# Small transfers of 5 to 15 rows in the load stream of a decode step, with sixteen more from GpSimd

## The chip, the cores and the metric

The kernel runs on one core of one Trainium2 chip. The metric is device time in microseconds (us), from the launch to the end on that core. The profile's "span" is the part of it from the first to the last instruction.

The engines are named as in the profile: PE is TensorE (matmul), PEld its weight load, DVE VectorE, ACT ScalarE, POOL GpSimd, SP SyncE. A "q" behind the name (SPq) is the engine's own instruction queue, from which it issues DMA transfers.

## The reference

One decode step of a layer with attention and a gated feed-forward side by side, for two sequences (B = 2), one token each, all in float32:

```
xn  = layernorm(x)                                   # x: 2 x 1 x 512
q   = xn @ wq                                        # 512 x 4096: 32 heads of 128
k,v = the last 4096 of 32768 positions of the caches # 8 key/value heads, 4 query heads to each
A   = softmax(q k^T / sqrt(128)) v @ wo              # wo: 4096 x 512
g,u = xn @ W_gate, xn @ W_up                         # 512 x 1792 each
B   = (g * (g > 0) * u) @ W_down                     # 1792 x 512
out = x + A + B
```

Every weight and every used cache row is read once. Key and value rows are 2 x 8 x 4096 x 128 floats each, 67.1 MB together; the weights are about 27.8 MB.

## The kernel before

**What is loaded.** The attention is cut into four groups g = 0 to 3 (NG): one sequence and four of its key/value heads each. A group's keys come in two loads of 4096 KB, a = 0 and 1, two heads each, and its values likewise. So there are eight loads `k{g}_{a}` and eight `v{g}_{a}`, made by `load_kv` (L108). The weights come as `wq0`, `wq1` (L75), `wg`, `wu` (L79), `wd` (L92: one large transfer and four of 64 KB, two of which go to the tile `wx`), `wo0` in one piece and `wo1` in four (L482 to L485).

**The ring.** All big loads go into one pool of four buffers (`ring`, RING = 4), in the order of the code, each into the buffer of the load four before it. `load` (L69) allocates the buffer and calls `nc.sync.dma_start`, so SyncE issues all of them, one after the other, into one DMA queue. SyncE first waits until the buffer's last reader is done: for a k buffer the last transpose (L302), for a v buffer the last matmul of L379. Only the input x (`x2`, L128) is loaded by ScalarE.

**The order of the loads** is that of the code, written out by hand (`manual_schedule`): x2, wq0, wq1, wg, wu; k0_0, k0_1; then k1_0, v0_0, k1_1, v0_1; k2_0, v1_0, k2_1, v1_1; k3_0, v2_0, k3_1, v2_1; then v3_0, v3_1, wd with its small parts, wo0, wo1. The framework puts in the waits: an instruction that touches a tile, or a part of it, waits for earlier ones that touch the same part, and the end of a transfer is told by a semaphore.

**The work on a load.** A k buffer is transposed on PE in blocks of 128 x 128 (`transposes`, L294, 64 of them), DVE and ACT copy the results out of PSUM in turn (L291), and `scores` (L308) multiplies with q. `softmax` (L321) of the group before runs between the transposes of the next group's first k load. `values` (L372) multiplies the probabilities with a v buffer, `gather` and `finish` put the heads together, and `project` (L464) accumulates the output from wd, then wo0 and wo1. One copy (L489) and one transfer (L490) end the kernel.

**GpSimd** sets constants up at the start (L90 to L183). Later it has one instruction, the memset of part of wd's tile (L98).

Of the kernel before, what the change touches and what calls it, by code (L numbers as in the profile page):

```python
# [9 lines left out]
F32 = mybir.dt.float32  # L10
# [10 lines left out]
def kernel(  # L21
# [12 lines left out]
    nc = tc.nc  # L34
# [14 lines left out]
    NG = B * R  # L49
# [9 lines left out]
    const = ctx.enter_context(tc.tile_pool(name="const", bufs=1))  # L59
# [9 lines left out]
    def load(name, src, shape):  # L69
        t = ring.tile(shape, F32, name=name, tag="ring")  # L70
        nc.sync.dma_start(t, src)
        return t
# [19 lines left out]
    def load_down():  # L92
# [12 lines left out]
                nc.sync.dma_start(dst[32 * h:32 * h + 16].rearrange("p s e -> p (s e)"), low)  # L105
        return t

    def load_kv(cache, name, g, a):  # L108
        r, b = divmod(g, B)
        base = cache[b, r * C + 2 * a, SK - W:SK, :]  # L110
        run = J * DH
        src = bass.AP(
            tensor=cache.tensor, offset=base.offset, ap=[[run, PK], [SK * DH, 2], [1, run]]
        )
        return load(f"{name}{g}_{a}", src, [P, run])
# [91 lines left out]
    for kc in range(KC):  # L207
        m, k = divmod(kc, 2)
# [7 lines left out]
    for kc in range(KC):  # L216
        for r in range(R):
            for c in range(C):
                n = r * C + c
# [214 lines left out]
    for a in range(NP):  # L434
        kwork(0, a, load_kv(k_cache, "k", 0, a))
    for g in range(1, NG):
        for a in range(NP):
            kt_in = load_kv(k_cache, "k", g, a)
            v_in = load_kv(v_cache, "v", g - 1, a)
            kwork(g, a, kt_in, [softmax(g - 1)] if a == 0 else [])  # L440
            if a:
                gather(g - 1, a - 1)
            elif g % B == 1 and g > 1:
                spread_heads((g - 2) // B)
            values(g - 1, a, v_in)
        gather(g - 1, NP - 1)
        finish(g - 1)
    g = NG - 1
# [70 lines left out]
```

## Time and profile before

| | us |
|---|---|
| median of 2 runs (231.06 to 231.21) | 231.13 |
| the profiled execution | 231.12 |
| its span | 229.3 |
| PE busy | 184.7 |
| DVE busy | 67.4 |
| ACT busy | 48.4 |
| POOL busy | 7.7 |
| mean granted TensorE clock | 0.933 of full speed |

Busy times count an engine's own work; waits and the issuing of transfers are not in them. The slices of the page give the busy share of an engine in tenths for each fortieth of the span, and for DMA the mean over the core's 16 DMA engines. In a list of waits a row reads: who waited, at which line, for whom, us in total, how many times, the longest. In an order of time a row reads: start, length, engine, line, operation, output and input, and how many instructions were put together in the row, so that its length reaches from the start of the first to the end of the last.

### The profile page before, as it was taken

The numbers are of one execution on the slowest core, as the hardware profiler recorded it, in microseconds if no ns is written. First come the engines' busy times: TensorE is split into PE (matmuls) and PEld (weight loads), VectorE is DVE, ScalarE is ACT, GpSimd is POOL, SyncE is SP. The second block draws the span as 40 slices with busy tenths as digits, with TensorE's granted clock in tenths as the row PEclk, the third lists the DMA queues.
The fourth block names the chain that finished last, engine by engine and source line by source line (L and its number), as shares of the span: only waits on it lengthen the run. The fifth ranks groups of instructions, "written<-read, shape, count | busy, mean of one in ns | idle before, by whom it ended". The sixth has DMA issues, their size and how long they took to land.

```text
span 229.3 us, 4136 instructions
## 1 busy us (share of the span) xinstructions
PE 184.7 (81%) x1868; PEld 112.5 (49%) x1868; DVE 67.4 (29%) x137; ACT 48.4 (21%) x81; POOL 7.7 (3%) x26
## 2 busy tenths in 40 slices
PE   0096753859999889998999799599999974988694
PEld 0061220239666573664574565338656532247582
DVE  0500101033544462441473341147224224001000
ACT  2000100004444461540252331025234202010000
POOL 8200000000000000000000000000000100000000
PEclk9999987575999999999999999979999998599979
DMA  7999999999899999999999999999999999999991
GB/s 275 457 412 415 465 400 432 434 457 443 383 449 452 410 412 457 432 406 437 452 417 410 452 423 437 423 446 423 414 446 426 429 429 437 418 440 420 409 369 51
DMA packets 3856, 95.15 MB, mean 415 GB/s; under 512 B 438, under 2 KB 446, under 8 KB 768
## 3 DMA queue, kind: packets, MB, share of 16 engines
q1 hardware_dynamic: 3836, 94.90, 96.7%
q8 instruction: 14, 0.23, 0.4%
q14 instruction: 2, 0.02, 0.0%
q10 hardware_dynamic: 4, 0.00, 0.0%
HBM read 94.90 MB, written 0.00 MB: 414 GB/s over the span
## 4 chain that ended last, share of the span: by engine, by line
PE 53%; DMA 34%; DVE 5%; POOL 2%; ACT 2%; issue 1%; SPq 0%; POOLq 0%
DMA k<-in_A_k_cache_dram 24%; PE pk L302 23%; PE s L315 11%; DMA wo<-in_A_wo_dram 10%; PE o L379 9%; PE q_ps L220 2%; PE pp L359 2%; PE xt_ps L210 2%; ACT p L348 2%; PE oa L395 2%; DVE kT L291 1%; PE y_ps L466 1%; PE op L409 1%; DVE on L291 1%; DVE pt L360 1%
## 5 line engine op out<-in xcount | busy, mean ns | idle before, releaser
L302 PE MATMUL pk<-ident,k 128*128 128x128 f32 x512 | 68.2, 287 | 4.8 <-DMA k<-in_A_k_cache_dram 4.8
L302 PEld LDWEIGHTS pk<-ident,k 128*128 128x128 f32 x512 | 58.1, 146 | 19.8 <-issue 15.6
L291 DVE COPY kT<-pk 128x512 f32<-128x512 f32 x64 | 44.2, 691 | 50.7 <-PE pk L302 40.7
L291 ACT COPY kT<-pk 128x512 f32<-128x512 f32 x64 | 37.5, 586 | 80.1 <-PE pk L302 80.1
L315 PE MATMUL s<-kT,qz 128*32 128x512 f32 x256 | 32.1, 617 | 0.0
L379 PE MATMUL o<-v,pt 128*32 128x512 f32 x256 | 32.0, 633 | 0.0
L379 PEld LDWEIGHTS o<-v,pt 128*32 128x32 f32 x256 | 11.2, 116 | 15.4 <-issue 10.7
L315 PEld LDWEIGHTS s<-kT,qz 128*32 128x32 f32 x256 | 7.2, 112 | 12.8 <-issue 12.4
L210 PE MATMUL xt_ps<-rep,xn 2*128 2x32 f32 x16 | 3.7, 400 | 11.1 <-DVE xn L204 11.1
L466 PE MATMUL y_ps<-wo,oT 128*17 128x128 f32 x256 | 9.6, 311 | 2.9 <-DMA wo<-in_A_wo_dram 2.5
L395 PE MATMUL oa<-on,pick 128*16 128x128 f32 x64 | 8.3, 273 | 4.1 <-DVE on L291 3.3
L291 DVE COPY on<-o 128x512 f32<-128x512 f32 x4 | 2.8, 691 | 30.0 <-PE o L379 30.0
L395 PEld LDWEIGHTS oa<-on,pick 128*16 128x16 f32 x64 | 5.8, 97 | 11.1 <-DVE on L291 7.0
L220 PE MATMUL q_ps<-wq,xnT 128*32 128x512 f32 x64 | 9.0, 716 | 2.5 <-DMA wq<-in_A_wq_dram 2.0
L466 PEld LDWEIGHTS y_ps<-wo,oT 128*17 128x17 f32 x256 | 7.9, 111 | 4.5 <-DMA wo<-in_A_wo_dram 3.4
L247 PE MATMUL u_ps<-wu,xnT 128*32 128x448 f32 x32 | 5.8, 908 | 4.7 <-DMA wu<-in_B_W_up_dram 4.7
L210 PEld LDWEIGHTS xt_ps<-rep,xn 2*128 2x128 f32 x16 | 3.6, 319 | 11.0 <-issue 11.0
L291 ACT COPY on<-o 128x512 f32<-128x512 f32 x4 | 2.3, 586 | 26.6 <-PE o L379 26.6
L348 ACT ACTIVATE p<-s,nm 128x1024 f32<-128x1024 f32 x4 | 4.5, 1115 | 12.6 <-DVE nm L343 12.5
L359 PE MATMUL pp<-ident,p 128*128 128x128 f32 x32 | 5.1, 289 | 2.4 <-ACT p L348 1.5
L247 PE MATMUL g_ps<-wg,xnT 128*32 128x448 f32 x32 | 4.9, 774 | 2.5 <-DMA wg<-in_B_W_gate_dram 2.5
L98 POOL MEMSET wd<- 64x1024 f32 x1 | 0.9, 945 | 171.5 <-PE pk L302 171.5
(80 smaller groups left out, 68.3 us busy)
## 6 DMA issues: line engine op xcount, KB each, us to landing
k<-in_A_k_cache_dram SPq DMA_DIRECT2D x8, 4096.0 KB, 26.6
v<-in_A_v_cache_dram SPq DMA_DIRECT2D x8, 4096.0 KB, 27.1
wq<-in_A_wq_dram SPq DMA_DIRECT2D x2, 4096.0 KB, 21.4
wo<-in_A_wo_dram SPq DMA_DIRECT2D x1, 4096.0 KB, 30.9
wg<-in_B_W_gate_dram SPq DMA_DIRECT2D x1, 3584.0 KB, 29.4
wu<-in_B_W_up_dram SPq DMA_DIRECT2D x1, 3584.0 KB, 38.6
wd<-in_B_W_down_dram SPq DMA_DIRECT2D x1, 3328.0 KB, 26.9
wo<-in_A_wo_dram SPq DMA_DIRECT2D x1, 2048.0 KB, 19.9
```

Of the source, the lines that this page charges most:

```text
L210: nc.tensor.matmul(xt_ps[:, o, kc, :], cols, rep.rearrange("r s b -> r (s b)"), start=True, stop=True)
L220: nc.tensor.matmul(q_ps[r][32 * c:32 * c + 32, :], xnT[:, 0, kc, :], wqt[kc // 2][:, kc % 2, n * 512:(n + 1) * 512], start=(kc == 0), stop ...
L247: nc.tensor.matmul(dst[32 * c:32 * c + 32, :], xnT[:, 1, kc, :], wt[:, kc, c * FQ:(c + 1) * FQ], start=(kc == 0), stop=(kc == KC - 1),)
L291: (nc.vector.tensor_copy if turn[0] % 2 else nc.scalar.copy)(dst, src)
L302: nc.tensor.transpose(pk[:, u * P:(u + 1) * P], kt_in[:, j * P:(j + 1) * P], ident)
L315: nc.tensor.matmul(ss[g][32 * q:32 * q + 32, :], qz[:, g, 32 * n:32 * n + 32], kt[:, h, q * 512:(q + 1) * 512], start=(a == 0 and s1 == 0 ...
L348: nc.scalar.activation(p, both, AF.Exp, bias=nm, scale=SCALE, accum_out=l)
L359: nc.tensor.transpose(pp[:, u], pv[:, lo:lo + P], ident)
L360: nc.vector.tensor_tensor(pts[g][:, jh].rearrange("p n u k -> p u n k"), pp.rearrange("p u (n k) -> p u n k", k=HK), own.rearrange("p h i ...
L379: nc.tensor.matmul(o[32 * q:32 * q + 32, :], pts[g][:, jh, n].rearrange("p u k -> p (u k)"), v[:, lo:lo + 512], start=(s1 == 0 and jh == 0 ...
L395: nc.tensor.matmul(oa[g], pick[:, u, 8 - 8 * a:24 - 8 * a], ons[a][:, u], start=(a == 0 and u == 0), stop=(a == NP - 1 and u == 3),)
L466: nc.tensor.matmul(y_ps[32 * e:32 * e + 17, :], lhsT.rearrange("p b s -> p (b s)")[:, 0:17], w[:, e * P:(e + 1) * P], start=False, stop=stop,)
```

## The change

Two small tiles are added, `marks` and `gmarks`, and a function `mark`, which `load_kv` calls ahead of seven of its loads: k0_0, k1_0, k2_0, k3_0, v2_0, v3_0 and v3_1. Each call issues eleven transfers on SyncE's queue, of 5, 6, ... 15 rows from wq into slots of their own in `marks`; a row has 2 to 12 floats, 8 to 48 bytes. The slots are the same at each of the seven calls. The third and the fifth call (ahead of k2_0 and of v2_0) issue eight more each from GpSimd, of two rows of 2 to 9 floats, into `gmarks`. That makes 77 transfers on SyncE and sixteen on GpSimd. No instruction reads the two tiles. Nothing else is changed.

```
+    marks = const.tile([16, 11, 12], F32, name="marks")
+    gmarks = const.tile([2, 8, 12], F32, name="gmarks")
+    at = [0]
+
+    def mark():
+        for k in range(5, 16):
+            nc.sync.dma_start(marks[0:k, k - 5, 0:k - 3], wq[0:k, 0:k - 3])
+        if at[0] in (2, 4):
+            for n in range(8):
+                nc.gpsimd.dma_start(gmarks[:, n, 0:2 + n], wq[0:2, 0:2 + n])
+        at[0] += 1
+
     def load_kv(cache, name, g, a):
+        if name == "k" and a == 0 or (name, g, a) in (("v", NG - 1, 0), ("v", NG - 1, 1), ("v", NG - 2, 0)):
+            mark()
         r, b = divmod(g, B)
         base = cache[b, r * C + 2 * a, SK - W:SK, :]
```

## The prediction

> **What bounds the kernel now.** I read the page first: the summary, the slices, the queues and the chain.
>
> ```profile
> span 229.3 us, 4136 instructions
> PE 184.7 (81%) x1868; PEld 112.5 (49%) x1868; DVE 67.4 (29%) x137; ACT 48.4 (21%) x81; POOL 7.7 (3%) x26
> ...
> DMA  7999999999899999999999999999999999999991
> ...
> q1 hardware_dynamic: 3836, 94.90, 96.7%
> ...
> PE 53%; DMA 34%; DVE 5%; POOL 2%; ACT 2%; issue 1%; SPq 0%; POOLq 0%
> ```
>
> The chain gives PE the larger share, but it runs through PE because PE frees the ring buffers; the slices say what sets the time. All 94.90 MB come in on SyncE's one queue (q1), whose packets fill 96.7% of the span. DMA stands at 9 in 37 of 40 slices. So an interval in which that queue is empty goes straight onto the end, unless the queue was idle there anyway, and it hardly ever is.
>
> Next the table of windows, for the steady rate, the start-up and the run-out of the stream. Its columns are length, busy time of PE, PEld, DVE, ACT and POOL, clock, DMA share and GB/s.
>
> ```profile
> 0.00:10.00 10.00, 0.00 (x0) 0.00 (x0) 2.49 (x13) 1.58 (x2) 6.74 (x25) 1.00 0.90 358
> 50.00:220.00 170.00, 153.04 (x1427) 97.59 (x1431) 59.35 (x103) 45.66 (x77) 0.94 (x1) 0.94 1.00 428
> 221.00:225.50 4.50, 3.83 (x132) 3.00 (x123) 0.00 (x0) 0.00 (x0) 0.00 (x0) 1.00 0.63 252
> ```
>
> The steady rate is 428 GB/s, so a 4096 KB load (4.19 MB) takes 9.8 us of the stream. In the same 170 us the stream brings 428 x 170 = 72.8 MB, 17.3 loads, for 153.0 us of PE: 8.8 us of PE for each load. PE is a tenth faster than the stream and waits for it.
>
> How far ahead the stream is fed stands among the DMA issues (KB each, us from issue to landing) and in SyncE's own waits.
>
> ```profile
> k<-in_A_k_cache_dram SPq DMA_DIRECT2D x8, 4096.0 KB, 26.6
> ...
> wu<-in_B_W_up_dram SPq DMA_DIRECT2D x1, 3584.0 KB, 38.6
> wd<-in_B_W_down_dram SPq DMA_DIRECT2D x1, 3328.0 KB, 26.9
> ```
>
> ```profile
> SPq L71 <- PE pk L302: 93.3, 9, 14.0
> ...
> SPq L485 <- DMA wd<-in_B_W_down_dram: 4.0, 1, 4.0
> ```
>
> A load lands 26.6 us after its issue and needs 9.8 us itself, so there are 1 to 2 loads in the queue ahead of it. SyncE mostly stands waiting for PE to free a buffer, and it can afford that as long as it isn't held until the queue has run out.
>
> The last row is the one that decides here. L485 issues the pieces of wo. SyncE's order in time:
>
> ```profile
> 178.95 0.53 SPq L97 DMA_DIRECT2D wd<-in_B_W_down_dram  x1
> 179.53 1.50 SPq L105 DMA_DIRECT2D wx<-in_B_W_down_dram  x2
> 181.07 1.30 SPq L105 DMA_DIRECT2D wd<-in_B_W_down_dram  x2
> ...
> 201.07 0.81 SPq L485 DMA_DIRECT2D wo<-in_A_wo_dram  x2
> ...
> 205.90 0.81 SPq L485 DMA_DIRECT2D wo<-in_A_wo_dram  x2
> ```
>
> The first two pieces of wo1 go out back to back at 201.07, the third only at 205.90, after a wait of 4.0 us on wd. wd landed at 178.95 + 26.9 = 205.85. The third piece has nothing to do with wd: another source, another ring buffer (wo1 takes that of v3_0). Number the SyncE and ScalarE transfers as the code issues them, x2 being 0: wd is 21, its four small parts 22 to 25, wo0 26, the pieces of wo1 27 to 30. The held piece is 29 = 21 + 8. Were the distance 7, the second piece would have been held; were it 9, the third would have gone and the fourth waited. I read this as eight completion semaphores used in turn: transfer n is not issued before transfer n - 8 has landed. Before the change that rule bites only here, since eight transfers are 40 to 80 us of stream. The Trainium skill, page "DMA: Bandwidth & Descriptors", section "Why a DMA increments its semaphore by 16 and not by 1", says that two transfers in flight on one semaphore can let a wait pass too early, and asks for one semaphore per slot in flight; the 4.0 us above agree with a program that keeps to that by waiting.
>
> **The change part by part.** *Eleven small transfers in front of a load.* Take the mark ahead of k2_0. Since the mark ahead of k1_0 the code has issued four loads: k1_0, v0_0, k1_1, v0_1. Call the old small ones s0 to s10, the loads L0 to L3, the new ones t0 to t10. Eight back from t0 to t3 stand s7 to s10; from t4 to t7 stand L0 to L3; from t8 to t10 stand t0 to t2. So t7 waits until L3, the last load issued, has landed, and then t7 to t10 and the next load must still be issued. All that is queued meanwhile is t0 to t6, a few hundred bytes each. The big stream runs dry.
>
> SyncE's first and last issues:
>
> ```profile
> 0.73 0.87 SPq L71 DMA_DIRECT2D wq<-in_A_wq_dram  x2
> ...
> 2.11 0.47 SPq L71 DMA_DIRECT2D wu<-in_B_W_up_dram  x1
> 20.70 16.01 SPq L71 DMA_DIRECT2D k<-in_A_k_cache_dram  x3
> ...
> 226.80 0.60 SPq L490 DMA_DIRECT2D out_dram<-yo  x1
> ```
>
> The other six go the same way, for t7 always stands eight behind the transfer just ahead of its mark, and that is always the last load issued. At k0_0 it is wu, landed at 2.11 + 38.6 = 40.7; before the change k0_0, k0_1 and k1_0 are issued from 20.70 to 36.71, all ahead of that. At k1_0 it is k0_1, at k3_0 v1_1, at v2_0 k3_0, at v3_0 v2_1, at v3_1 v3_0. Each time four small issues and the load remain behind the wait. Seven marks, seven dry queues.
>
> The windows up to the landings of wu and wd, and the end of out:
>
> ```profile
> 0.00:40.70 40.70, 18.82 (x120) 8.02 (x120) 5.84 (x25) 2.69 (x4) 6.74 (x25) 0.94 0.97 412
> 0.00:205.85 205.85, 167.91 (x1452) 98.59 (x1452) 65.85 (x133) 48.35 (x81) 7.68 (x26) 0.93 1.00 426
> ```
>
> ```profile
> SPq L514 <- DMA out_dram<-yo: 0.8, 1, 0.8
> ```
>
> One dry queue costs, in terms:
> - *The run-out.* The 16 engines don't finish a load together. At the end of the kernel, with nothing behind, 4.50 us at 252 GB/s moved 1.13 MB, 2.65 us of work at 428: 1.85 us lost. That is the nearest row. Bounds: nothing, if the engine that is last stays last and so loses no time of its own; 3.4 us from wd, for by its landing at 205.85 the stream had moved 426 x 205.85 = 87.7 MB, 1.45 MB beyond wd's end at 86.2 MB (two wq, two gate and up, 16 loads and wd), bytes that would have had no place in a dry queue. For wu the same sum gives 16.77 - 15.73 = 1.04 MB, 2.4 us.
> - *SyncE's wake-up.* From 205.85 to 205.90: 0.05 us.
> - *Four issues.* The four small parts of wd took 1.50 + 1.30 = 2.80, 0.70 each; the pieces of wo 0.81 for two, 0.41 each; out 0.60. I take 0.65, a simple pattern but few rows: 2.6 us. Bounds 1.6 (0.41) and 2.8 (0.70).
> - *The wait of t8 for t0.* t0 to t2 sit in the queue right behind L3 and should land while t7 is issued: nothing. At most one landing of a small transfer, as out's: 0.60 + 0.8 = 1.4 us.
> - *The load's own start.* By 10 us the stream had moved 3.58 MB, 8.36 us of work; it began in effect at 1.64, after an issue at 0.73: 0.91 us.
>
> Sum: 1.85 + 0.05 + 2.6 + 0 + 0.91 = 5.4 us. Between 0 + 0.05 + 1.6 + 0.91 = 2.6 and 3.4 + 0.05 + 2.8 + 1.4 + 0.91 = 8.6.
>
> *What lies behind.* After a restart the stream must not starve again. Three of the four ring buffers hold loads that PE has had time for (8.8 us each against 9.8 of stream), so the next loads follow 0.5 us apart; were PE one load behind, the second would be issued 8.8 us late, still before the first has landed (0.91 + 9.8). PE gets nothing new during a gap and cannot shorten it later, for the bytes still come at 428 GB/s. The tail behind the last load is as before: the pieces of wo wait for v3_1 and wd as now, while wo0 (9.8 us) is in the stream.
>
> *The data of the small transfers.* 110 rows of 8 to 48 bytes per mark, lying in the dry interval: nothing more. The four 64 KB parts of wd tell the same in the full stream:
>
> ```profile
> 185.14 0.34 SPq L485 DMA_DIRECT2D wo<-in_A_wo_dram  x1
> ```
>
> ```profile
> wo<-in_A_wo_dram SPq DMA_DIRECT2D x1, 4096.0 KB, 30.9
> ```
>
> wo0 landed at 185.14 + 30.9 = 216.04, 10.2 us after wd, for 4.46 MB that need 10.4 at 428. Four small transfers between them left no mark. The same skill page, section "Anatomy of one DMA", fits about 2.0 us plus bytes over 436 GB/s to one transfer; by it, as an estimate, 77 in a line would take 154 us, and these four 8 us, which this trace does not show.
>
> *GpSimd's sixteen.* No transfer of GpSimd is in the trace. They stand in its queue behind the set-up and ahead of one instruction only:
>
> ```profile
> 178.98 0.94 POOL L98 MEMSET wd<- 64x1024 f32 x1 [171.52 <-PE pk L302]
> ```
>
> Idle for 171.5 us, GpSimd can spend 1.4 us (out's row) on each, 22 us in a line, and be done at about 30. The engines carry 32 short rows more. I take nothing; with that cover gone it would be at most 22.
>
> Total: 7 x 5.4 = 37.8 us on the profiled execution's 229.3 us span: 267. Around its span that execution has 231.12 - 229.3 = 1.8 us, and the median of the runs is 231.13, so **269 us**. Bounds of this case: 231.1 + 7 x 2.6 = 249 and 231.1 + 7 x 8.6 = 291.
>
> **Rivals.** *Not slower: the small transfers don't wait.* The 4.0 us hold comes from something else that this one place has, a limit on rows in flight for instance, which small transfers would not reach. Then a mark costs SyncE 11 x 0.65 = 7.2 us of issuing, and of the 26.6 us of lead of a load 26.6 - 9.8 - 7.2 = 9.6 are left: hidden. Time 231 to 232. It decides as soon as SyncE's hold ends at least one load (9.8 us) before the queue is empty. For it: one hold is thin evidence. Against it: its end, 0.05 us behind a landing, and the distance of eight.
>
> *Slower still: one after another.* If each small transfer is issued only once the one before it has landed, since all write one tile, a mark costs 1.85 + 0.05 + 11 x 1.4 + 0.91 = 18.2 us, seven 127: 358 us. With their 1.4 us in the queue one by one and no run-out, it is 77 x 1.4 = 108: 339. Against both: the parts of wd (two into wx, two into the tile that wd's main transfer was still filling) followed each other within 0.1 us of an issue's end.
>
> **How the numbers follow.** Seven dry queues: 0.84. Not slower: 0.09. One after another: 0.07. The likeliest gives 269. Its bounds, 249 to 291, hold nearly all of its 0.84; I round up to 293 for GpSimd's transfers, and stop there, since the rivals lie far off on both sides. Within 2% is about what a measurement of this kernel can tell from no change; that is most of the first rival, 0.08, faster 0.01, and the rest, 0.91, slower.
>
> **What would show it.** Right: seven intervals of DMA at or near zero in the windows, each just ahead of one of the seven loads, 4 to 7 us with its run-out; in SyncE's waits, small transfers waiting for DMA k, v and wu, up to 20 us or more each; loads behind a mark that land after about 11 us instead of 26.6; GB/s as now in between. Wrong on size: a run-out below 1 us or above 3, or small issues away from 0.65. Wrong altogether: SyncE's waits still mostly on PE pk, with DMA at 9 throughout; or waits of a small transfer on another of the same mark. GpSimd's part is wrong if its transfers end later than 30 us or the DMA share dips beside them.

## The result, and the profile after

| | before | after |
|---|---|---|
| median, us | 231.13 | 271.94 (271.51 to 272.36) |
| profiled execution, us | 231.12 | 271.51 |
| its span, us | 229.3 | 269.5 |
| mean granted TensorE clock | 0.933 | 0.88 |

The changed kernel takes 1.1768 times as long (95% interval 1.1749 to 1.1787), 40.8 us more. The forecast was 269 us, with a range of 249 to 293.

The changed kernel's page, the same rows as before; below the queue of SyncE (q1) is the new one of GpSimd (q0):

```profile
span 269.5 us, 4236 instructions
PE 191.4 (71%) x1868; PEld 116.1 (43%) x1868; DVE 67.4 (25%) x137; ACT 48.3 (18%) x81; POOL 16.1 (6%) x42
...
DMA  8999974995699999299999929399993877999991
...
q1 hardware_dynamic: 5376, 94.93, 84.0%
...
q0 software_dynamic: 512, 0.00, 0.1%
...
DMA 82%; PE 13%; SPq 4%; issue 1%; DVE 0%
```

The slices show it at once: the row of nines has holes. The q1 share fell from 96.7 to 84.0%, while the megabytes are the same: 0.967 x 229.3 = 221.7 us of packets before, 0.840 x 269.5 = 226.4 now. So 35.5 of the 40.2 us of longer span are time in which the queue, as a mean over the 16 engines, had no packet under way; its packets themselves took 4.7 us more. The chain no longer runs through PE: 82% of it is DMA, and 4% SyncE's own issuing, which was 0.

The waits of SyncE's queue in the changed kernel (us in total, times, longest), where L115 is the line of the small transfers:

```profile
SPq L115 <- DMA v<-in_A_v_cache_dram: 66.8, 7, 10.9
SPq L115 <- DMA k<-in_A_k_cache_dram: 64.9, 8, 10.7
...
SPq L115 <- DMA wq<-in_A_wq_dram: 18.4, 2, 9.5
SPq L71 <- PE pk L317: 9.9, 5, 7.6
SPq L115 <- DMA wu<-in_B_W_up_dram: 9.3, 1, 9.3
```

Before, the first row was SyncE waiting for PE to free buffers, 93.3 us; that is 9.9 now. Small transfers wait for loads they have nothing to do with.

One dry queue, the one ahead of k2_0. SyncE's order in time, then the windows around it (length, PE, PEld, DVE, ACT, POOL, clock, DMA share, GB/s):

```profile
112.00 1.54 SPq L115 DMA_DIRECT2D marks<-in_A_wq_dram  x4
113.64 0.55 SPq L71 DMA_DIRECT2D k<-in_A_k_cache_dram  x1
```

```profile
108.00:109.00 1.00, 1.00 (x16) 0.19 (x8) 0.00 (x0) 0.17 (x1) 0.00 (x0) 1.00 1.24 524
109.00:110.00 1.00, 1.00 (x10) 0.67 (x7) 0.00 (x0) 0.00 (x0) 0.00 (x0) 1.00 0.21 67
110.00:110.70 0.70, 0.70 (x8) 0.62 (x6) 0.62 (x1) 0.20 (x1) 0.00 (x0) 1.00 0.12 47
110.70:112.00 1.30, 1.30 (x13) 1.18 (x12) 0.81 (x3) 0.87 (x2) 0.00 (x0) 1.00 0.00 0
112.00:113.64 1.64, 1.64 (x16) 1.11 (x18) 1.34 (x2) 0.94 (x3) 0.00 (x0) 1.00 0.02 1
113.64:114.80 1.16, 1.16 (x16) 0.36 (x9) 0.00 (x0) 0.34 (x1) 0.00 (x0) 1.00 0.03 1
114.80:115.80 1.00, 1.00 (x15) 0.70 (x14) 0.00 (x0) 0.00 (x0) 0.00 (x0) 1.00 1.76 524
```

These rows must be read with care. A window books a packet where it starts, with all its bytes and its whole length; that is how the last row comes to a share of 1.76 of the 16 engines. A load's packets are 32 KB each and last 1.2 us in the trace. So the 47 GB/s of the third row, 0.033 MB, are one packet, and it runs on into the row of zeros.

From 109.0 the last packets of v0_1 straggle in. By the trace's own packets the last three end at 110.60, 111.17 and 111.71. At 112.00, 0.29 us after the last, SyncE is free, and exactly four small transfers go out, t7 to t10, and at 113.64 the load. Its first packet starts at 114.98, 1.34 us after its issue. All the while PE still works on what it has.

The chain in order of time has four more of them: a load lands, four issues on L115 (in pieces of one), the load. One of the four at k3_0 is long, 1.66 us; more on that below.

```profile
2.11 39.02 DMA wu<-in_B_W_up_dram
...
41.15 0.30 SPq L115
...
42.81 13.82 DMA k<-in_A_k_cache_dram
...
119.58 36.78 DMA v<-in_A_v_cache_dram
...
157.12 1.66 SPq L115
...
159.31 12.83 DMA k<-in_A_k_cache_dram
...
175.09 32.24 DMA v<-in_A_v_cache_dram
...
209.00 12.39 DMA v<-in_A_v_cache_dram
...
223.84 19.59 DMA wd<-in_B_W_down_dram
```

The other two, at k1_0 and v2_0, are not on the chain but stand in SyncE's order in the same way. To price all seven, count each packet's bytes evenly over its length and set them against 428 GB/s: the holes cost 4.4 to 6.6 us each, 39.5 of the 40.2 us together. Nothing is left for the lower mean clock to explain.

Between two holes the stream is as fast as ever:

```profile
118.00:152.00 34.00, 25.86 (x215) 15.62 (x208) 11.88 (x21) 8.71 (x15) 0.00 (x0) 0.90 1.00 430
```

The built program names its semaphores, and there the rule that the prediction read out of one 4.0 us wait stands in full: eight of them, taken in turn (the order of SyncE's instructions with their waits, cut).

```
L71 DMA k1_0 [waits DMAHW5,PE]
L71 DMA v0_0 [waits DMAHW6,PE]
L71 DMA k1_1 [waits DMAHW7,PE]
L71 DMA v0_1 [waits DMAHW0,PE]
L115 DMA marks 5x2 [waits DMAHW1]
...
L115 DMA marks 12x9 [waits DMAHW0]
```

The transfer of 12 rows, the eighth of the mark, needs the semaphore of v0_1.

### The profile page after: what moved, and what is told of

It reads as the page before. It is cut to its first block, busy times and chain, and to the rows that moved or that the text cites. A ratio compares the mean times of both kernels' runs of the same rounds, so it can differ in the third digit from the quotient of the medians.

```text
span 269.5 us, 4236 instructions
## 1 busy us (share of the span) xinstructions
PE 191.4 (71%) x1868; PEld 116.1 (43%) x1868; DVE 67.4 (25%) x137; ACT 48.3 (18%) x81; POOL 16.1 (6%) x42
## 4 chain that ended last, share of the span: by engine, by line
DMA 82%; PE 13%; SPq 4%; issue 1%; DVE 0%
DMA v<-in_A_v_cache_dram 30%; DMA k<-in_A_k_cache_dram 22%; DMA wu<-in_B_W_up_dram 14%; PE pk L317 8%; DMA wo<-in_A_wo_dram 8%; DMA wd<-in_B_W_down_dram 7%; SPq L115 3%; PE s L330 2%; PE o L394 1%; SPq L71 1%; PE y_ps L481 0%; PE oa L410 0%; DVE yo L504 0%; SPq L97 0%
## 5 line engine op out<-in xcount | busy, mean ns | idle before, releaser
L317 PE MATMUL pk<-ident,k 128*128 128x128 f32 x512 | 71.0, 295 | 29.2 <-DMA k<-in_A_k_cache_dram 29.2
L317 PEld LDWEIGHTS pk<-ident,k 128*128 128x128 f32 x512 | 61.0, 151 | 44.8 <-issue 40.8
L394 PE MATMUL o<-v,pt 128*32 128x512 f32 x256 | 34.1, 671 | 3.4 <-DMA v<-in_A_v_cache_dram 3.4
L330 PE MATMUL s<-kT,qz 128*32 128x512 f32 x256 | 33.4, 639 | 0.0
L394 PEld LDWEIGHTS o<-v,pt 128*32 128x32 f32 x256 | 10.9, 121 | 21.3 <-issue 14.1
L118 POOL DMA_DIRECT2D gmarks<-in_A_wq_dram x16 | 8.4, 531 | 13.0 <-DMA gmarks<-in_A_wq_dram 13.0
L262 PE MATMUL u_ps<-wu,xnT 128*32 128x448 f32 x32 | 4.9, 782 | 4.6 <-DMA wu<-in_B_W_up_dram 4.6
L374 PE MATMUL pp<-ident,p 128*128 128x128 f32 x32 | 5.7, 316 | 2.4 <-ACT p L363 1.5
```

The lines of the kernel that those rows point to most:

```text
L118: nc.gpsimd.dma_start(gmarks[:, n, 0:2 + n], wq[0:2, 0:2 + n])
L262: nc.tensor.matmul(dst[32 * c:32 * c + 32, :], xnT[:, 1, kc, :], wt[:, kc, c * FQ:(c + 1) * FQ], start=(kc == 0), stop=(kc == KC - 1),)
L317: nc.tensor.transpose(pk[:, u * P:(u + 1) * P], kt_in[:, j * P:(j + 1) * P], ident)
L330: nc.tensor.matmul(ss[g][32 * q:32 * q + 32, :], qz[:, g, 32 * n:32 * n + 32], kt[:, h, q * 512:(q + 1) * 512], start=(a == 0 and s1 == 0 ...
L374: nc.tensor.transpose(pp[:, u], pv[:, lo:lo + P], ident)
L394: nc.tensor.matmul(o[32 * q:32 * q + 32, :], pts[g][:, jh, n].rearrange("p u k -> p (u k)"), v[:, lo:lo + 512], start=(s1 == 0 and jh == 0 ...
```

## The experiments

Each kernel still computes the whole reference; only the small transfers differ. The theory is the prediction's: a transfer is not issued before the one eight places ahead has landed, so a mark of seven or more runs the queue dry. Rivals: the small transfers have a price of their own in the queue; GpSimd's carry part of the loss; a small transfer waits for the earlier one to the same slot; odd row counts hold the queue. The ratios below are against runs of the kernel before on the same chip.

**Six small transfers, and seven.** The theory has a sharp step where the rivals have a slope.

```
-        for k in range(5, 16):
+        for k in range(5, 11):      # seven: range(5, 12)
...
-        if at[0] in (2, 4):         # GpSimd's, left out here and in all below but one
```

> Six small transfers per mark (5 to 10 rows, 42 in all) instead of eleven, and none from GpSimd. Theory (a transfer is not issued before the one eight places ahead has landed, so a mark of seven or more lets the queue run dry): with six, the load behind a mark stands eight behind the last load but one, so SyncE is free while a whole load (9.8 us) is still queued. No dry queue: 231 to 233 us. Rival (each small transfer has a price of its own in the queue, 40.8 us / 77 = 0.53 us): 231.1 + 42 x 0.53 = 253 us. Rival (GpSimd's sixteen carry part of the loss): anything between.

> Seven small transfers per mark (5 to 11 rows, 49 in all), none from GpSimd: one more than six. Theory: now the load behind a mark stands eight behind the last load issued, and SyncE waits for its landing: seven dry queues, but with no small transfer left to issue in them. Each costs what the changed kernel's does less its four small issues, 5.8 - 1.8 = 4.0 us: 231.1 + 28 = 259 us (256 to 262). The step from six to seven is then some 27 us. Rival (a price per small transfer): 231.1 + 49 x 0.53 = 257 us, but only 4 us above six.

Six: 234.51 us, ratio 1.0135 (1.0118 to 1.0153). Seven: 258.35 us, 1.1180 (1.1146 to 1.1213). One more transfer of 11 rows per mark costs 23.8 us; the first six cost 3.3 together. The slices of six have no hole. Here they are with a row of its waits, in which loads (L71) wait for loads, and the same two of seven:

```profile
DMA  7999999999999999999999999999999999999960
```

```profile
SPq L71 <- DMA k<-in_A_k_cache_dram: 51.5, 6, 9.4
```

```profile
DMA  8999994996799999499999959499994959999991
```

```profile
SPq L71 <- DMA v<-in_A_v_cache_dram: 37.6, 4, 9.7
```

SyncE waits for landings in both, and for about as long, 9.4 and 9.7 us at most. In six one load is still queued when the wait ends; in seven none is. That settles the mechanism, and it prices a dry queue in which nothing but the load is issued: (258.35 - 231.20) / 7 = 3.9 us, what six loses included. Six came out above its 231 to 233; more on that below.

**The same 77, spread.**

```
-        if name == "k" and a == 0 or (name, g, a) in (("v", NG - 1, 0), ...):
-            mark()
+        mark()
...
-        for k in range(5, 16):
+        for i in range(5 if at[0] < 13 else 4):
+            k = 5 + (5 * at[0] + i) % 11
```

> All 77 small transfers of SyncE, of the same shapes, spread evenly: five (at the last three loads four) ahead of each of the sixteen key and value loads, none from GpSimd. Theory: with five between two loads, SyncE waits at most for the load before the last one, one load is always queued, and nothing runs dry: 231 to 234 us. Rival (a price per small transfer, or of odd row counts, or of rewriting the same slots): as the changed kernel, about 272 us.

235.93 us, 1.0186 (1.0156 to 1.0216): 4.7 us for the transfers that cost 40 when they stood in seven heaps. What they are is a small part of the loss; where they stand is the rest. Here too the time lies above the expectation.

**The same 77, from GpSimd.**

```
-            nc.sync.dma_start(marks[0:k, k - 5, 0:k - 3], wq[0:k, 0:k - 3])
+            nc.gpsimd.dma_start(marks[0:k, k - 5, 0:k - 3], wq[0:k, 0:k - 3])
```

> The 77 small transfers issued by GpSimd instead of SyncE, at the same places of the code; its own sixteen are left out. Theory: SyncE's order is as before the change, and GpSimd's transfers only wait for each other: 231 to 235 us, the upper end if GpSimd, at about 2.3 us for each, reaches the memset of wd's tile only near 185 us and holds SyncE there. Rival (the DMA engines pay for the small transfers, whoever issues them): about 272 us.

233.38 us, 1.0097 (1.0081 to 1.0113). GpSimd does wait for its own, mostly 1.9 us between two of them, but has issued the last by 161.3 us and sits idle for 19 us before the memset:

```profile
159.60 0.52 POOL L115 DMA_DIRECT2D marks<-in_A_wq_dram  x1 [1.93 <-DMA marks<-in_A_wq_dram]
160.82 0.52 POOL L115 DMA_DIRECT2D marks<-in_A_wq_dram  x1 [0.71 <-DMA marks<-in_A_wq_dram]
180.40 0.94 POOL L98 MEMSET wd<- 64x1024 f32 x1 [19.05 <-PE pk L314]
```

**SyncE's part and GpSimd's part alone.** One kernel leaves out GpSimd's sixteen, the other SyncE's 77.

> The changed kernel without GpSimd's sixteen transfers; SyncE's 77 stay. Theory: GpSimd's are finished early and hold nobody up: 270 to 272 us, as the changed kernel. Rival (GpSimd's carry part of the loss): 265 us or less.

> Only GpSimd's sixteen transfers, none of SyncE's. Theory: 231 to 232 us, at most the 0.03 us each that the 77 on GpSimd showed (2.2 us in all). Rival (GpSimd's carry part of the loss): 235 us or more.

SyncE's alone: 271.09 us, 1.1728 (1.1710 to 1.1747). GpSimd's alone: 231.45 us, 1.0013 (1.0003 to 1.0022), 0.4 us. GpSimd carries next to nothing.

**Slots of their own.** The 77 write `marks` at the same places seven times, which could be a wait in itself.

```
-    marks = const.tile([16, 11, 12], F32, name="marks")
+    marks = const.tile([112, 11, 12], F32, name="marks")
-            nc.sync.dma_start(marks[0:k, k - 5, 0:k - 3], wq[0:k, 0:k - 3])
+            nc.sync.dma_start(marks[16 * at[0]:16 * at[0] + k, k - 5, 0:k - 3], wq[0:k, 0:k - 3])
```

> SyncE's 77 as in the changed kernel, but each mark writes rows of its own (partitions 16 further on), so no transfer overwrites an earlier one's data; none from GpSimd. Theory (turns of eight): the waits stay, 270 to 272 us. Rival (a transfer waits for the earlier one to the same slot): the waits and the dry queues go, 231 to 236 us.

270.97 us, 1.1718 (1.1697 to 1.1738), as with shared slots. The rewriting costs nothing that these runs show.

**Sixteen rows each.**

```
-            nc.sync.dma_start(marks[0:k, k - 5, 0:k - 3], wq[0:k, 0:k - 3])
+            nc.sync.dma_start(marks[:, k - 5, 0:k - 3], wq[0:16, 0:k - 3])
```

> Eleven small transfers per mark, but each of 16 rows (2 to 12 floats) instead of 5 to 15, none from GpSimd. Theory (turns of eight): row counts don't matter, 270 to 272 us, a little more or less as the issue of a 16-row transfer is longer or shorter than 0.41 us. Rival (row counts that do not fill the sixteen engines hold the queue): 231 to 240 us.

272.16 us, 1.1778 (1.1763 to 1.1793). Row counts are not the cause.

**Fifteen small transfers.** Four more issues in each dry queue, to weigh the issue term by itself.

```
-        for k in range(5, 16):
+        for i in range(15):
+            k = 5 + i % 11
```

> Fifteen small transfers per mark (rows 5 to 15, then 5 to 8 again, in slots of their own; 105 in all), none from GpSimd. Theory: still seven dry queues, now with eight small issues at 0.41 us in each instead of four: 272 + 7 x 1.65 = 283.5 us (282 to 285). The load behind the mark now stands eight behind the small transfer that ended the wait; if that one's landing takes longer than seven issues (2.9 us), up to 1 us per mark more, 290. Rival (dry queues cost the same however many issues lie in them, being bound by something else): 272 to 274 us.

279.94 us, 1.2101 (1.2081 to 1.2121): 8.85 us above SyncE's 77, 1.26 per mark, where 1.65 was expected. The issues in a dry queue cost time, as the theory has it, but the four more were cheaper than the four that were there. SyncE's order in time, of fifteen and of the kernel with SyncE's 77 alone:

```profile
115.42 2.90 SPq L116 DMA_DIRECT2D marks<-in_A_wq_dram  x8
118.41 0.54 SPq L71 DMA_DIRECT2D k<-in_A_k_cache_dram  x1
```

```profile
111.83 1.54 SPq L115 DMA_DIRECT2D marks<-in_A_wq_dram  x4
113.47 0.55 SPq L71 DMA_DIRECT2D k<-in_A_k_cache_dram  x1
```

From the first small issue to the load 2.99 us against 1.64: 1.35 for four, 0.34 each. The added ones have 5 to 8 rows; those of 12 to 15 rows take 0.41. My price was that of the wrong rows. The wait for a landing that I feared on top did not show in the time.

**Four and five: where six's 3.3 us come from.**

> Four small transfers per mark (5 to 8 rows, 28 in all), none from GpSimd. With four, each load waits for the load four before it, which its buffer makes it do anyway; the queue is as deep as before the change. Asked: where six's 3.3 us come from. If from a price of each small transfer in a full queue (3.3 / 42 = 0.08 us): 231.1 + 2.2 = 233.3 us. If from the shallower queue (one load ahead instead of two or three): 231 to 232 us.

> Five small transfers per mark (5 to 9 rows, 35 in all), none from GpSimd: two loads stay queued while SyncE waits. By a price of each small transfer: 231.1 + 35 x 0.08 = 233.9 us. By the depth of the queue: as four, 231 to 232 us, and the step comes between five and six.

Four: 232.32 us, 1.0053 (1.0039 to 1.0066). Five: 233.80 us, 1.0115 (1.0102 to 1.0128). Per small transfer that is 1.26 / 28 = 0.045 us for four, 2.74 / 35 = 0.078 for five, 3.3 / 42 = 0.079 for six, 4.7 / 77 = 0.061 for spread and 2.2 / 77 = 0.028 from GpSimd. Neither answer fits alone: a price for each should not nearly double from four to five, and a depth of the queue does not explain the 1.26 us of four, or GpSimd's 2.2, whose queue is as deep as before. The kept traces add one thing. Counted by packets, six is 1.4 us behind the kernel before when 92 MB have come in, but 3.2 us behind when the last data have; for five these are 1.0 and 2.5, for spread 2.5 and 4.9, for the 77 from GpSimd 1.9 and 2.7. So 1.5 to 2.4 us of the loss of five, six and spread arise in the last 3 MB, after the last of the small transfers. The slices of six show it too: they end in 6 and 0, those of the kernel before in 9 and 1. Why the stream runs out more slowly was not tried. In all these kernels the loss is at most 5 us.

## Why the prediction was right, point by point

- **The bound.** Right: time without packets in the one queue went onto the end, 35.5 of the 40.2 us. Nothing was given back; between holes the rate is 430 GB/s, as it was.
- **The rule of eight.** Right, and the basis of all else. Its evidence was one wait of 4.0 us whose end and distance could be counted; the step from six to seven shows it at work.
- **Seven dry queues, four issues and the load behind each.** Right at each place.
- **The price of one, 5.4 us.** The span grew by 40.2 / 7 = 5.7 per mark. That the forecast came so near is in part luck, for two terms were off in opposite directions. The terms one by one:
  - *The load's own start* is the term that failed. It was put at 0.91, without bounds; at the seven marks 2.0 to 2.7 us were lost there, 2.0 at k2_0. The 0.91 rests on the row 0.00:10.00, which books 3.58 MB; by the trace's packets only 3.19 MB had come in by then, for the row counts in full what had only begun. The difference is 0.9 us of the stream, and with it the term would have been 1.8.
  - *Four issues* were put at 2.6 us and took 1.64 at k2_0, 1.6 to 1.8 at six of the seven marks: I took 0.65 from the four small parts of wd, a pattern of more dimensions with 4 KB rows, and the small ones take 0.41; an issue away from 0.65 was among the signs of being wrong on size. My bounds for the term, 1.6 to 2.8, hold these six.
  - *The run-out* was put at 1.85 and lost 0.6 to 2.2 us, 2.2 at k2_0. That includes 0.3 to 0.7 us between the last data and SyncE's next issue, of which *SyncE's wake-up* had only 0.05.
  - *The wait of t8 for t0*, taken as nothing, did not come. The long issue at k3_0, 157.12 1.66, looks like it, but SyncE's list of waits has none there, and the small transfer eight places ahead had landed at 156.50. It falls together with a packet of the instruction queue (q8), 157.15 to 158.39; that this held it is not shown.

  With the terms as measured at k2_0 the sum is 2.2 + 1.64 + 2.0 = 5.8; the means over the seven marks are 1.7, 1.9 and 2.1.
- **The time of a load behind a mark.** Said to be about 11 us. k3_0 and v3_0, alone in the queue, took 12.83 and 12.39, or 2.6 to 3.0 more than the 9.8 of stream. Of that some 2.0 us are lost at the start, where I had put 0.91, and the rest at the end, which I had left out of that figure though it was in the sum. The Trainium skill, page "DMA: Bandwidth & Descriptors", section "Anatomy of one DMA — SWDGE (gpsimd) path", puts about 2.0 us of fixed cost on a transfer that GpSimd issues, most of it the confirmation that the last byte has landed. The prediction held that figure against SyncE's transfers, for which the section does not give it. For a load alone in SyncE's queue the traces show the larger part at the start: 1.3 to 2.0 us from the issue to the first packet at the seven marks, against 0.3 to 0.7 us from the last data to SyncE's next issue.
- **SyncE's waits.** Said to reach 20 us or more; the longest is 10.9. From t4 on each small transfer waits for one load, so SyncE wakes at every landing and goes back to waiting.
- **GpSimd's sixteen.** Nothing, said I; 0.4 us, the runs say. The last is issued at 28.33, near the estimate, but it lands only at 41.6 by the trace, and an end later than 30 us was the prediction's own sign that this part is wrong. The price of 1.4 us each, one after the other, was not how it went: 0.52 to issue, eight in flight at a time, and a wait of up to 1.9 us for the one eight places ahead (below). The idle time of 171.5 us was cover enough all the same.
- **The data of the small transfers.** In the dry interval they are hidden, as said. In a full queue I said nothing as well; there they cost 0.03 to 0.08 us each with whatever else changed.
- **The rivals.** "Not slower" fell with the waits named after the loads. "One after another" fell with 1.54 us for four of them.

## What to carry to other kernels

When a framework hands out a fixed number of completion semaphores in turn, count transfers, not bytes: with eight, seven small transfers between two loads on SyncE's queue, here of less than 1 KB each, are enough to empty the stream, for 3.9 us, and eleven for 5.7. Spread small transfers so that a big load always remains queued behind the wait, or issue them from GpSimd, whose transfers had waits of their own and left SyncE's order alone (233.4 us against 271.1). A single odd wait in the profile, one that names a transfer the waiting instruction has no business with, is worth the counting: it told the mechanism of the whole change. And take no time of a microsecond out of a table of windows, since packets of 1.2 us are booked where they start: that is how the load's start came out at half its size.

## What the runs showed of the hardware that was not expected

A load that finds SyncE's queue empty starts its first packet 1.3 to 2.0 us after its issue, and 0.3 to 0.7 us pass between a load's last data and SyncE's next issue (the seven marks of the changed kernel). A transfer of two rows from GpSimd lands late when the load stream is running. The DMA issues of the changed kernel and of the one with all 77 on GpSimd (KB each, median us from issue to landing), and GpSimd's order in the changed kernel:

```profile
gmarks<-in_A_wq_dram POOLq DMA_DIRECT2D x2, 0.0 KB, 11.2
...
gmarks<-in_A_wq_dram POOLq DMA_DIRECT2D x2, 0.1 KB, 15.1
```

```profile
marks<-in_A_wq_dram POOLq DMA_DIRECT2D x7, 0.0 KB, 16.8
```

```profile
7.42 4.27 POOL L118 DMA_DIRECT2D gmarks<-in_A_wq_dram  x8
13.39 0.52 POOL L118 DMA_DIRECT2D gmarks<-in_A_wq_dram  x1 [1.69 <-DMA gmarks<-in_A_wq_dram]
...
28.33 0.52 POOL L118 DMA_DIRECT2D gmarks<-in_A_wq_dram  x1 [1.62 <-DMA gmarks<-in_A_wq_dram]
```

That is 11 to 17 us for less than a kilobyte, against 1.4 us for the output's transfer at the quiet end of the kernel. Most of it is waiting behind GpSimd's own transfers. Eight go out back to back and the ninth once the first has landed, so GpSimd takes turns of eight as SyncE does. The first, with none ahead of it, lands 5.7 us after its issue, the eighth 16.9. With all 77 on GpSimd one lands every 2.2 us on average, and eight such turns make 17.5 us. Why one takes that long beside the stream was not tried.
